# Moving the query projections of an attention stage ahead, and its output transfers to GpSimd's DMA queue

## The chip, the cores and the metric

The kernel runs on one core of a Trainium2 chip. Its engines are TensorE (PE; its weight loads are shown apart as PEld), VectorE (DVE), ScalarE (ACT), GpSimd (POOL) and SyncE (SP), which here only issues DMAs. Each engine executes its own instructions in order and waits at semaphores for the others. The metric is the time of one execution on the device in microseconds, as a median of several runs.

## The reference

Two stages follow one another. The first is attention without a softmax: queries and keys are sketched into 64 features, which are products of two projections to 8 each. The second is a mixture of eight experts whose routing weights come from eight Sinkhorn iterations.

```python
# q, k, v: (4 batches, 4 heads, 1088, 32); S1, S2: (8, 32)
def phi(x):
    a = np.einsum('rd,bhsd->bhsr', S1, x)
    b = np.einsum('rd,bhsd->bhsr', S2, x)
    return np.einsum('bhsi,bhsj->bhsij', a, b).reshape(*x.shape[:-1], 64)
q_p, k_p = phi(q), phi(k)
kv = np.einsum('bhsf,bhsd->bhfd', k_p, v)
z = np.sum(k_p, axis=2)
num = np.einsum('bhsf,bhfd->bhsd', q_p, kv)
den = np.einsum('bhsf,bhf->bhs', q_p, z)[..., None] + 1e-06
x = (num / den)               # -> (4352, 128): one row for each batch and position

logits = x @ w_gate           # (4352, 8)
P = np.exp(logits - logits.max())
for _ in range(8):            # rows, then columns
    P /= P.sum(1, keepdims=True) + 1e-09
    P /= P.sum(0, keepdims=True) + 1e-09
    P *= N / E
for e in range(8):            # w1[e]: 128 x 1024, w2[e]: 1024 x 128
    out += P[:, e:e + 1] * (np.maximum(x @ w1[e], 0.0) @ w2[e])
```

All is in float32.

## The kernel before

The experts' matrix products make up most of the work, and they are cut into small steps. A generator `steps()` puts out one step at a time, and `fill(n)` takes steps from it until about n units of work are out; a step on 480 columns counts as one unit, one on 256 columns as 0.53. The attention is put out piece by piece with calls of `fill` between the pieces, so that TensorE has expert work while the attention waits for VectorE, ScalarE or a DMA. The order on TensorE and VectorE is the order of these calls. Experts 0 and 1 are applied without routing weights to some of the rows at first (their results are weighted later); these steps need only x.

Step by step, the order from the start is as follows (cut to what matters):

```python
with tc.manual_schedule(engines={engines.DVE, engines.PE, engines.Activation}):
    ...
    transpose_k(0)
    keys_ab(0)                    # projects the keys
    ...
    keys_sums(0)
    multiply(0)
    transpose_q(0, chunks[0][1])
    keys_kept(0)
    query_products(1)
    fractions(0)
    multiply(1)
    divide(0)                     # writes x of batch 0, columns 0 to 384
    fractions(1)
    query_products(2)
    divide(1)
with tc.manual_schedule(engines={engines.DVE, engines.PE}):
    fill(1)
    multiply(2)
    fractions(2)
    fill(1)
    transpose_q(1)
    queries_ab(1)
    repeat_a(1)
    repeat_b(1)
    fill(1)
    divide(2)
    fill(1)
    transpose_k(1)
    load_k(2)
    load_q(2)
    load_v(2)
    fill(1)
    keys_ab(1)
    fill(1.5)
    keys_products(1, 0)
    fill(1.5)
    keys_products(1, 1)
    fill(1.5)
    keys_products(1, 2)
    fill(1.5)
    for b in range(1, B):
        for n, _ in zip((1.4,) * (9 if b + 1 < B else 5), attention(b), strict=True):
            fill(n)
    for n in routing():           # begins with fill(5), then the logits of all batches
        fill(n)
```

Batches 1 to 3 take their queries a longer way. They are transposed (VectorE), projected (TensorE, 12 matmuls; line 418), copied from PSUM (ScalarE; line 421), written to DRAM repeated (tiles qa and qb, two and four DMAs; lines 425 and 429), and read back into ph (four DMAs; line 434) and rb (one DMA; line 437), so that one elementwise product of ph and rb makes the 64 features:

```python
def transpose_q(b, lo=0, hi=S):
    nc.vector.transpose(out=qT[:, lo:hi], in_=loaded["q", b]...[:, lo:hi])      # L288

def queries_ab(b):
    ...
    x = qT.rearrange("p (h q c t s) -> p h c t q s", h=2, q=2, c=3, t=3)
    for cs in ((0, 1), (2,)):
        ...
        nc.tensor.matmul(...)                                                   # L418
        nc.scalar.copy(ab[:, cs[0]:cs[-1] + 1], pq)                             # L421
    ...
    nc.sync.dma_start(out=qa[:, :, s], in_=x)                                   # L425, two of them
    ...
    nc.sync.dma_start(out=qb[h, :, :, s]..., in_=x)                             # L429, four

def repeat_a(b):
    for j in range(4):
        nc.sync.dma_start(out=phs[b % 2][j::4], in_=queries[b][0]...)           # L434

def repeat_b(b):
    nc.sync.dma_start(out=rb, in_=queries.pop(b)[1]...)                         # L437

def times(b, c):
    ph = third(phs[b % 2], c)
    nc.vector.tensor_tensor(ph, ph, third(rb, c), op=Alu.mult)                  # L444
```

The attention of one batch from 1 on, with the output's way: `tops` multiplies features and key sums (L453), `over` divides and transposes (L466 to L472), and `take_over` turns the result into the layout of x through DRAM:

```python
def take_over(b, lo, hi):
    xd = dram.tile([P, H, hi - lo], F32, name=f"xd{b}{lo}")
    nc.sync.dma_start(out=xd, in_=turned[b][:, :, lo:hi])                       # L477
    for h in range(H):
        nc.sync.dma_start(out=xT[32 * h:32 * (h + 1), ...], in_=xd...[h])       # L479

def attention(b):
    follows = b + 1 < B
    keys_sums(b)
    times(b, 0)
    if follows:
        transpose_q(b + 1)
    yield
    keys_kept(b)
    if follows:
        queries_ab(b + 1)
        repeat_a(b + 1)
    times(b, 1)
    tops(b, 0)
    yield
    times(b, 2)
    if follows:
        repeat_b(b + 1)
    over(b, 0)
    tops(b, 1)
    yield
    over(b, 1)
    if b + 1 == B:
        take_over(b, 0, 192)
    yield
    tops(b, 2)
    if follows:
        transpose_k(b + 1)
    ...                           # loads of batch b + 2
    yield
    over(b, 2)
    ...                           # take_over of the rest, then the keys of batch b + 1
```

The keys are transposed into kT (L292, L294) and projected from there (L303, L307). The expert work's first layer is L889, its second L1062; L906 and L951 are VectorE's sums between the two. The logits' matmuls are L487. PSUM tiles named "a" rotate through four banks.

Of the kernel before, what the change touches and what calls it, by code (L numbers as in the profile page):

```python
# [10 lines left out]
F32 = mybir.dt.float32  # L11
# [39 lines left out]
def kernel(  # L51
# [12 lines left out]
    nc = tc.nc  # L64
    P = nc.NUM_PARTITIONS
    B, H, S, D = q.shape
# [58 lines left out]
    xT = big.tile([P, N + 2 * 32], F32, name="xT")  # L125

    W9 = 9 * 32
    qT = wk.tile([P, 4 * W9], F32, name="qT", bufs=1)
    nc.gpsimd.memset(qT[:, S:], 0.0)
    kT = wk.tile([P, S], F32, name="kT", bufs=1)  # L130

    phs = [wk.tile([P, 2, 4 * W9], F32, name=f"ph{i}", bufs=1) for i in range(2)]
    rb = wk.tile([P, 2, 4 * W9], F32, name="rb", bufs=1)

    lgT = qT[:, 0:S].rearrange("p (a s) -> p a s", s=32)
    lgp = kT.rearrange("p (a e) -> p a e", e=32)
    pT = dram.tile([E, N], F32, name="pT")


# [24 lines left out]
    def load_q(b):  # L164
        qx = ld.tile([P, SA, D], F32, tag="q", name="qx")
        nc.sync.dma_start(out=qx, in_=q[b].rearrange("h (s a) d -> (h s) a d", a=SA))
        loaded["q", b] = qx

    def load_v(b):
        vx, o = v_slots[b % 2], v[b].offset  # L170
        for c in range(4):
            nc.sync.dma_start(
                out=vx[32 * c:32 * (c + 1), 0:H, 0:NT, :].rearrange("p h t d -> p h (t d)"),
                in_=AP(tensor=v.tensor, offset=o + NT * D * c, ap=[[SA * D, 32], [S * D, H], [1, NT * D]]))
        for c in range(2):
            nc.sync.dma_start(
                out=vx[32 * c:32 * (c + 1), 0:H, NT, :],
                in_=AP(tensor=v.tensor, offset=o + (4 * NT + c) * D, ap=[[SA * D, 32], [S * D, H], [1, D]]))

    load_k(0)  # L180
    load_q(0)
    load_v(0)

    def load_w(e, sums=True, again=False):
        w1 = wpool.tile([P, F], F32, tag="w1", name="w1")
# [92 lines left out]
    nc.gpsimd.memset(wg, 0.0)  # L278
    nc.sync.dma_start(out=wg[:, 0:E], in_=moe_w_gate)
    first_w = load_w(0)  # L280
    load_q(1)
    load_v(1)


    keys, queries = {}, {}

    def transpose_q(b, lo=0, hi=S):
        nc.vector.transpose(out=qT[:, lo:hi], in_=loaded["q", b].rearrange("p a d -> p (a d)")[:, lo:hi])  # L288

    def transpose_k(b):  # L290
        kx = loaded["k", b]
# [79 lines left out]
    def multiply(c):  # L371
        lo, hi = chunks[c]
        for i, pb in enumerate(queries[0, c]):
            nc.vector.tensor_tensor(phs[0][:, i, lo:hi], phs[0][:, i, lo:hi], pb, op=Alu.mult)
# [34 lines left out]
    def queries_ab(b):  # L409
        qa = dram.tile([H * R, 2, 2, 2 * W9], F32, name=f"qa{b}")  # L410
        qb = dram.tile([2, R, 2 * R, 2, 2 * W9], F32, name=f"qb{b}")
        ab = wk.tile([P, 3, 192], F32, tag="qab", name="qab", bufs=1)
        x = qT.rearrange("p (h q c t s) -> p h c t q s", h=2, q=2, c=3, t=3)
        for cs in ((0, 1), (2,)):
            pq = bank()[:, 0:192 * len(cs)].rearrange("p (c n) -> p c n", n=192)
            for i, c in enumerate(cs):
                for s in range(2):
                    nc.tensor.matmul(pq[64 * s:64 * (s + 1), i].rearrange("p (t q s) -> p t q s", t=3, q=2),  # L418
                                     wdq.rearrange("p n f -> p (n f)"), x[:, s, c], start=True, stop=True,
                                     tile_position=(0, 64 * s))  # L420
            nc.scalar.copy(ab[:, cs[0]:cs[-1] + 1], pq)  # L421
        abf = ab.rearrange("p c n -> p (c n)")
        for s in range(2):
            x = abf[64 * s:64 * s + 32].unsqueeze(1).to_broadcast([32, 2, 2 * W9])
            nc.sync.dma_start(out=qa[:, :, s], in_=x)  # L425
        for s in range(2):
            for h in range(2):
                x = abf[64 * s + 32 + h:64 * (s + 1):2].unsqueeze(1).to_broadcast([2 * R, R, 2 * W9])
                nc.sync.dma_start(out=qb[h, :, :, s].rearrange("i f n -> f i n"), in_=x)  # L429
        queries[b] = qa, qb  # L430

    def repeat_a(b):
        for j in range(4):
            nc.sync.dma_start(out=phs[b % 2][j::4], in_=queries[b][0].rearrange("(x r) j s n -> (r j) x (s n)", x=2))  # L434

    def repeat_b(b):
        nc.sync.dma_start(out=rb, in_=queries.pop(b)[1].rearrange("h i (j x) s n -> (h i j) x (s n)", x=2))  # L437
# [4 lines left out]
# [4 lines that stand above are left out]
    def tops(b, c):  # L446

        pn = bank()[:, 0:3 * H * (D + 1)].rearrange("p (t h d) -> p t h d", t=3, h=H)
        ph = third(phs[b % 2], c)
        for t in range(3):  # L450
            for i in range(2):
                for s in range(2):
                    nc.tensor.matmul(pn[64 * s:64 * (s + 1), t, 2 * i:2 * i + 2].rearrange("p h d -> p (h d)"),  # L453
                                     ph[:, i, s, 64 * t:64 * (t + 1)], kvs[b % 2][:, i].rearrange("p h d -> p (h d)"),
                                     start=(t == 0 and i == 0), stop=False, tile_position=(0, 64 * s))
        for s in range(2):
            nc.tensor.matmul(pn[64 * s:64 * (s + 1), :, :, D], ones[:, 0:64], eps, start=False, stop=True,
                             tile_position=(0, 64 * s))
        queries[b, c] = pn
# [14 lines left out]
    def take_over(b, lo, hi):  # L474

        xd = dram.tile([P, H, hi - lo], F32, name=f"xd{b}{lo}")
        nc.sync.dma_start(out=xd, in_=turned[b][:, :, lo:hi])  # L477
        for h in range(H):
            nc.sync.dma_start(  # L479
                out=xT[32 * h:32 * (h + 1), b * S:b * S + 4 * W9].rearrange("d (f n) -> d f n", f=4)[:, :, lo:hi],  # L480
                in_=xd.rearrange("(f d) h n -> h d f n", f=4)[h])

# [15 lines left out]
    def attention(b):  # L498


        follows = b + 1 < B
        keys_sums(b)
        times(b, 0)
        if follows:
            transpose_q(b + 1)
        yield
        keys_kept(b)
        if follows:
            queries_ab(b + 1)
            repeat_a(b + 1)  # L510
        times(b, 1)
        tops(b, 0)
        yield
        times(b, 2)
        if follows:
            repeat_b(b + 1)
        over(b, 0)
# [8 lines that stand above are left out]
            transpose_k(b + 1)  # L526
        if b + 2 < B:
            load_k(b + 2)
            load_q(b + 2)
            load_v(b + 2)  # L530
        yield
        over(b, 2)
        if b + 1 < B:
            take_over(b, 0, W9)
        else:
            take_over(b, 192, W9)
        if follows:
            keys_ab(b + 1)
            yield
            keys_products(b + 1, 0)  # L540
            yield
            keys_products(b + 1, 1)
            yield
            keys_products(b + 1, 2)
            yield
# [589 lines left out]
    with tc.manual_schedule(engines={engines.DVE, engines.PE, engines.Activation}):  # L1135
        st = projections()
        transpose_k(0)
        keys_ab(0)
        repeated(st)
        load_k(1)  # L1140
        transpose_q(0, 0, chunks[0][1])
        query_products(0)
        for part_ in range(3):
            keys_products(0, part_)
        keys_sums(0)
        multiply(0)
        transpose_q(0, chunks[0][1])
        keys_kept(0)
        query_products(1)
        fractions(0)  # L1150
        multiply(1)
        divide(0)
        fractions(1)
        query_products(2)
# [3 lines that stand above are left out]
        multiply(2)  # L1158
        fractions(2)
        fill(1)  # L1160
        transpose_q(1)
        queries_ab(1)
        repeat_a(1)
        repeat_b(1)
        fill(1)
        divide(2)
        fill(1)
        transpose_k(1)
        load_k(2)
        load_q(2)  # L1170
        load_v(2)
        fill(1)
        keys_ab(1)
        fill(1.5)
        keys_products(1, 0)
        fill(1.5)
        keys_products(1, 1)
        fill(1.5)
        keys_products(1, 2)
        fill(1.5)  # L1180
        for b in range(1, B):
            for n, _ in zip((1.4,) * (9 if b + 1 < B else 5), attention(b), strict=True):
                fill(n)
        for n in routing():
            fill(n)
        early.close()
        pools.append(ctx.enter_context(tc.tile_pool(name="late", bufs=2)))
        prepare_x(PLAIN)
        fill(8)
# [32 lines left out]
```

## Time and profile before

| | us |
|---|---|
| time, median of 3 runs | 940.04 |
| lowest and highest | 938.84, 941.04 |
| span of the profiled execution | 935.3 |
| TensorE busy | 914.8 |
| VectorE busy | 696.3 |
| ScalarE busy | 416.6 |
| GpSimd busy | 195.9 |

In the profile, a line of a timeline gives the start and the length in microseconds, the engine, the line of the kernel, the operation, the tiles written and read, and how many instructions were merged into it; in square brackets stands the idle time ahead of it and what ended that. SPq stands for SyncE's queue of DMA issues. In a list of waits, the numbers are the total, the count and the longest. The row of slices cuts the span into 40 equal parts and gives the busy share of each in tenths. The mean granted clock of TensorE is 0.998. The attention occupies the first 122 us, the routing the time to about 185 us, and from there the weighted expert work runs to the end.

### The profile page before, as it was taken

How to read it: one execution, taken by the hardware profiler on the slowest of the kernel's cores; microseconds unless marked ns; L12 is line 12 of the kernel's file. 1: busy time of each engine (PE TensorE's matmuls, PEld its weight loads, DVE VectorE, ACT ScalarE, POOL GpSimd, SP SyncE). 2: the span in 40 equal slices, each digit the busy share in tenths (PEclk: the TensorE clock that was granted, in tenths of full speed). 3: DMA queues.
4: the chain of work that ended last, by engine and by line, in shares of the span. 5: the costliest groups of instructions: out<-in, count | busy, mean ns of one | idle time of the engine just before them, and what ended most of it. 6: DMA issues, size and time to landing. Idle time of an engine off the chain costs nothing.

```text
span 935.3 us, 18858 instructions
## 1 busy us (share of the span) xinstructions
PE 914.8 (98%) x7434; PEld 556.6 (60%) x7434; DVE 696.3 (74%) x1200; ACT 416.6 (45%) x901; POOL 195.9 (21%) x182
## 2 busy tenths in 40 slices
PE   8888999999999999999999999999999999999997
PEld 6676634666666666665555555555555555556864
DVE  7687769978788788586876656965757977768655
ACT  2544345564444454434544444544445444445443
POOL 2010000073665501130020101201110343321210
PEclk9999999999999999999999999999999999999999
DMA  7896300123335545354354534364434446442640
GB/s 216 226 290 166 113 21 1 26 105 108 107 109 170 172 148 151 121 174 142 117 154 121 179 107 148 111 182 131 140 115 152 151 150 204 160 167 92 183 140 12
DMA packets 93208, 128.14 MB, mean 137 GB/s; under 512 B 25376, under 2 KB 71456, under 8 KB 88384
## 3 DMA queue, kind: packets, MB, share of 16 engines
q1 hardware_dynamic: 91888, 126.78, 43.8%
q8 instruction: 58, 0.95, 0.4%
q10 hardware_dynamic: 1232, 0.16, 0.1%
q14 instruction: 30, 0.25, 0.1%
HBM read 107.88 MB, written 19.05 MB: 136 GB/s over the span
## 4 chain that ended last, share of the span: by engine, by line
PE 90%; DVE 8%; issue 1%; ACT 1%; POOL 0%; DVEq 0%; ACTq 0%; POOLq 0%
PE a L889 47%; PE s L1062 40%; DVE hb L906 2%; PE a L335 1%; PE a L114 1%; PE a L303 0%; PE a L453 0%; DVE rs L582 0%; DVE ph L444 0%; DVE p L585 0%; DVE cs L588 0%; DVE kp L319 0%; DVE kept L715 0%; DVE w L718 0%; DVE kT L292 0%
## 5 line engine op out<-in xcount | busy, mean ns | idle before, releaser
L889 PE MATMUL a<-xe,w 128*64 128x256 f32 (+1 forms) x2560 | 517.5, 470 | 0.0
L893 ACT ACTIVATE hb<-a 128x256 f32<-128x256 f32 (+5 forms) x408 | 194.9, 479 | 253.5 <-PE a L889 225.0
L893 ACT ACTIVATE hx<-a 128x256 f32<-128x256 f32 (+1 forms) x360 | 167.1, 464 | 213.9 <-PE a L889 194.1
L889 PEld LDWEIGHTS a<-xe,w 128*64 128x64 f32 x2560 | 206.8, 137 | 79.8
L1062 PE MATMUL s<-hb,ws 128*64 128x256 f32 (+4 forms) x1344 | 237.8, 395 | 2.4 <-DVE hb L906 1.6
L1062 PE MATMUL s<-hx,ws 128*64 128x256 f32 x1280 | 204.8, 379 | 0.6 <-DVE kept L718 0.6
L951 DVE TENSOR_TENSOR hb<-hb 128x512 f32<-128x512 f32 (+1 forms) x204 | 133.4, 665 | 93.9 <-ACT hb L893 89.8
L951 DVE TENSOR_TENSOR hx<-hx 128x512 f32<-128x512 f32 (+1 forms) x204 | 153.3, 761 | 66.3 <-ACT hx L893 61.1
L658 POOL TENSOR_TENSOR xe<-xT,xe 128x768 f32<-128x768 f32 (+2 forms) x41 | 85.1, 2076 | 554.5 <-DMA xe<-pT 401.6
L1062 PEld LDWEIGHTS s<-hb,ws 128*64 128x64 f32 x1344 | 113.8, 137 | 110.6 <-issue 80.0
L1062 PEld LDWEIGHTS s<-hx,ws 128*64 128x64 f32 x1280 | 105.9, 137 | 99.7 <-issue 74.4
L889 PE MATMUL a<-xT,w 128*64 128x480 f32 (+4 forms) x512 | 119.4, 463 | 3.7 <-DVE hb L906 2.5
L1062 PE MATMUL s<-hb,w 128*64 128x256 f32 (+4 forms) x496 | 101.9, 410 | 0.0
L906 DVE TENSOR_TENSOR hb<-hb 128x480 f32<-128x480 f32 (+8 forms) x96 | 64.2, 670 | 21.1 <-ACT hb L893 13.6
L1062 PE MATMUL s<-hx,w 128*64 128x256 f32 x384 | 68.3, 379 | 0.0
L889 PEld LDWEIGHTS a<-xT,w 128*64 128x64 f32 x512 | 50.5, 137 | 26.6 <-issue 14.2
L238 POOL TENSOR_TENSOR ws<-w 128x256 f32<-128x256 f32 (+1 forms) x70 | 60.1, 892 | 13.6 <-PE a L889 8.7
L1062 PEld LDWEIGHTS s<-hb,w 128*64 128x64 f32 x496 | 45.8, 137 | 22.8 <-issue 8.1
L906 DVE TENSOR_TENSOR hx<-hx 128x256 f32<-128x256 f32 (+1 forms) x65 | 39.1, 607 | 24.5 <-ACT hx L893 23.4
L951 DVE TENSOR_TENSOR pqg<-hb 128x512 f32<-128x512 f32 x68 | 48.8, 759 | 0.0
L1062 PEld LDWEIGHTS s<-hx,w 128*64 128x64 f32 x384 | 34.0, 137 | 10.9 <-DVE hx L906 0.3
L951 DVE TENSOR_TENSOR pqg<-hx 128x512 f32<-128x512 f32 x68 | 35.8, 566 | 0.0
(164 smaller groups left out, 468.8 us busy)
## 6 DMA issues: line engine op xcount, KB each, us to landing
w<-in_moe_w_dram SPq DMA_DIRECT2D x82, 512.0 KB, 5.0
ws<-ws SPq DMA_DIRECT2D x34, 1024.0 KB, 4.9
xe<-pT SPq DMA_DIRECT2D x34, 384.0 KB, 4.0
ws<-ws SPq DMA_DIRECT2D x12, 512.0 KB, 4.9
qb<-qab SPq DMA_DIRECT2D x12, 288.0 KB, 4.2
ph<-qa SPq DMA_DIRECT2D x12, 288.0 KB, 4.4
rb<-qb SPq DMA_DIRECT2D x3, 1152.0 KB, 8.0
pb<-pT SPq DMA_DIRECT2D x6, 384.0 KB, 6.7
```

The source lines that it names most:

```text
L114: nc.tensor.matmul(warm[:, 0:P], ones, ones, start=True, stop=True)
L238: tc.keep_in_program_order(nc.gpsimd.tensor_tensor(ws[:, c:c + len(ns)], blocks(x), blocks(y), op=Alu.subtract if off else Alu.add))
L335: nc.tensor.matmul(pv[64 * s:64 * (s + 1), i], kp[0:n, H * t + h].rearrange("p i j -> p (i j)"), vx[0:n, slots[h], t, :], start=(t == 0 an ...
L658: tc.keep_in_program_order(nc.gpsimd.tensor_tensor(out, x, pb, op=Alu.mult))
L889: nc.tensor.matmul(ph[sl], loaded_w[j][0][:, P * f + H2 * s:P * f + H2 * (s + 1)], sources[j][:, lo:hi], start=True, stop=True, tile_posit ...
L893: nc.scalar.activation(out=out, in_=ph, func=Act.Relu)
L906: nc.vector.tensor_tensor(out, a, b, op=Alu.subtract)
L951: nc.vector.tensor_tensor(out if not isinstance(out, tuple) else places(*out), places(*a), places(*b) if isinstance(b, tuple) else b, op=A ...
L1062: nc.tensor.matmul(sums[g][i][H2 * s:H2 * (s + 1), n * place:n * (place + 1)], w, x, start=c == 1, stop=c == per, tile_position=(0, H2 * s))
```

## The change

Every batch's queries are projected earlier, and the output of the attention is moved by another queue.

- Batch 1's queries are loaded ahead of the first expert weights, transposed during batch 0 and put into kT, the keys' buffer, which is free at that time. They are projected, and their repeated copies sent on their way, between batch 0's second multiplication and its first division.
- Batch 2's queries are transposed after batch 1's first `tops` and projected after its third `times`, instead of at the start of that attention. Batch 3's follow later in batch 1's attention, between the products of batch 2's keys, instead of in batch 2's.
- x is carried by DMAs that GpSimd issues, not SyncE.
- The calls of `fill` before the attention of batch 1 come to 7.5 units instead of 11, and the keys of batch 1 are transposed ahead of the last division of batch 0.

The aim is to have the repeated queries in place when they are wanted, and to keep x's transfers from standing in SyncE's queue behind DMAs that wait.

```diff
-    qT = wk.tile([P, 4 * W9], F32, name="qT", bufs=1)
-    nc.gpsimd.memset(qT[:, S:], 0.0)
-    kT = wk.tile([P, S], F32, name="kT", bufs=1)
+    qT, kT = (wk.tile([P, 4 * W9], F32, name=n, bufs=1) for n in ("qT", "kT"))
+    for t in (qT, kT):
+        nc.gpsimd.memset(t[:, S:], 0.0)
 ...
     load_v(0)
+    load_q(1)
 ...
     first_w = load_w(0)
-    load_q(1)
     load_v(1)
 ...
     def transpose_q(b, lo=0, hi=S):
-        nc.vector.transpose(out=qT[:, lo:hi], in_=...)
+        to = kT if b == 1 else qT
+        nc.vector.transpose(out=to[:, lo:hi], in_=...)
 ...
-        x = qT.rearrange("p (h q c t s) -> p h c t q s", h=2, q=2, c=3, t=3)
+        x = (kT if b == 1 else qT).rearrange("p (h q c t s) -> p h c t q s", h=2, q=2, c=3, t=3)
 ...
-        nc.sync.dma_start(out=xd, in_=turned[b][:, :, lo:hi])
+        nc.gpsimd.dma_start(out=xd, in_=turned[b][:, :, lo:hi])
         for h in range(H):
-            nc.sync.dma_start(
+            nc.gpsimd.dma_start(
 ...                                    # attention(b)
         times(b, 0)
-        if follows:
-            transpose_q(b + 1)
         yield
         keys_kept(b)
-        if follows:
-            queries_ab(b + 1)
-            repeat_a(b + 1)
         times(b, 1)
         tops(b, 0)
+        if b == 1:
+            transpose_q(2)
         yield
         times(b, 2)
+        if b == 1:
+            queries_ab(2)
+            repeat_a(2)
         if follows:
             repeat_b(b + 1)
 ...
             load_k(b + 2)
-            load_q(b + 2)
             load_v(b + 2)
 ...
             keys_products(b + 1, 0)
+            if b == 1:
+                transpose_q(3)
             yield
             keys_products(b + 1, 1)
+            if b == 1:
+                queries_ab(3)
+                repeat_a(3)
 ...                                    # the order from the start
         keys_kept(0)
+        transpose_q(1)
         query_products(1)
         fractions(0)
         multiply(1)
+        queries_ab(1)
+        load_q(2)
+        repeat_a(1)
+        repeat_b(1)
         divide(0)
 ...
         fractions(2)
         fill(1)
-        transpose_q(1)
-        queries_ab(1)
-        repeat_a(1)
-        repeat_b(1)
-        fill(1)
-        divide(2)
-        fill(1)
         transpose_k(1)
         load_k(2)
-        load_q(2)
         load_v(2)
+        load_q(3)
+        divide(2)
+        fill(1.5)
+        keys_ab(1)
         fill(1)
-        keys_ab(1)
-        fill(1.5)
         keys_products(1, 0)
-        fill(1.5)
+        fill(1)
         keys_products(1, 1)
-        fill(1.5)
+        fill(1)
         keys_products(1, 2)
-        fill(1.5)
+        fill(1)
```

More of the change, by code (lines that the diff above doesn't have):

```diff
@@ L135 @@
     lgT = qT[:, 0:S].rearrange("p (a s) -> p a s", s=32)
-    lgp = kT.rearrange("p (a e) -> p a e", e=32)
+    lgp = kT[:, 0:S].rearrange("p (a e) -> p a e", e=32)
     pT = dram.tile([E, N], F32, name="pT")
@@ L287, in transpose_q @@
     def transpose_q(b, lo=0, hi=S):
-        nc.vector.transpose(out=qT[:, lo:hi], in_=loaded["q", b].rearrange("p a d -> p (a d)")[:, lo:hi])
+        to = kT if b == 1 else qT
+        nc.vector.transpose(out=to[:, lo:hi], in_=loaded["q", b].rearrange("p a d -> p (a d)")[:, lo:hi])
     def transpose_k(b):
```

## The prediction

> **What bounds the kernel now.** I read the page's busy times first, then its row of slices, then TensorE's waits by stretch, and only then the timelines of the stretches in which TensorE stood still.
>
> ```profile
> PE 914.8 (98%) x7434; PEld 556.6 (60%) x7434; DVE 696.3 (74%) x1200; ACT 416.6 (45%) x901; POOL 195.9 (21%) x182
> PE   8888999999999999999999999999999999999997
> DMA  7896300123335545354354534364434446442640
> ```
>
> TensorE is idle for 935.3 - 914.8 = 20.5 us in all. The chain that ended last runs through TensorE for 90% of the span. Asked in stretches, TensorE has no idle time from 230 to 900 us and loses 7.6 us of 36 in the tail; neither is touched. Everything that the change moves lies before 130 us, where the slices (23.4 us each) show 8s. The number of matmuls stays the same, so the change can only give back idle time. The list of waits from 40 to 125 us holds all of it there:
>
> ```profile
> PE a L889 <- DVE hb L906: 2.5, 1, 2.5
> PE a L303 <- DVE kT L294: 1.4, 1, 1.4
> PE a L453 <- ACT qab L421: 1.3, 1, 1.3
> PE a L418 <- ACT f L736: 1.2, 1, 1.2
> ```
>
> That is 6.4 us; from 20 to 40 us there are 0.86 (for the second piece of x of batch 0), 0.2 and 0.89 us (for the keys' transpose) more. So about 8 us, 0.9% of 940, is the ceiling. The releasers named are the last by time, not always the cause. Three timelines show the causes (VectorE, then SyncE's queue; columns are start, length, what):
>
> ```profile
> 43.84 0.96 DVE L444 TENSOR_TENSOR ph<-ph,rb 128x768 f32<-128x768 f32 x1 [5.28 <-DMA rb<-qb]
> 44.72 1.30 DVE L288 STREAM_TRANSPOSE qT<-qx 128x1088 f32<-128x1088 f32 x1
> ```
> ```profile
> 67.72 0.34 SPq L477 DMA_DIRECT2D xd<-xt  x1
> 77.52 0.60 SPq L425 DMA_DIRECT2D qa<-qab  x1
> 78.23 2.41 SPq L479 DMA_DIRECT2D xT<-xd  x4
> ...
> 116.05 0.55 SPq L477 DMA_DIRECT2D xd<-xt  x1
> 118.57 1.74 SPq L479 DMA_DIRECT2D xT<-xd  x4
> ```
> ```profile
> 83.73 1.03 PE L889 MATMUL a<-xT,w 128*64 128x480 f32 x4 [2.55 <-DVE hb L906]
> ...
> 122.02 2.24 PE L487 MATMUL a<-xT,wg 128*32 128x384 f32 x24
> ```
>
> VectorE sits 5.28 us for the repeated queries of batch 1 (rb) to land. Then the transpose for batch 2's queries stands ahead of everything else, ends at 46.02, and the projection (L418) starts at 46.17: its 1.25 us is this transpose's, not ScalarE's. The products after it (L453, at 48.67) wait for the copy of the key sums, which VectorE ends at 48.57. On SyncE's queue, x of batch 1 leaves for DRAM at 67.72, and the four DMAs that bring it back go out only at 78.23: ahead of them stands an issue that waits 9.5 us for qab. They land 3.2 us after the last one, issued at 80.2, which is 83.5, and the first matmul on batch 1's x starts at 83.73. So this wait of 2.55 us is x's, though the view names hb.
>
> **What the skill says.** "Perfetto Trace Analysis", section Optimization Strategy, says to look for gaps on the contended engine and follow each to the semaphore behind it; this trace agrees in so far as all the gaps above lead to VectorE's order or to SyncE's. "DMA: Bandwidth & Descriptors", section Issuing engines are not separate DMA queues, says that another issuing engine gets no bandwidth of its own, only saves issue time. In the trace the 9.5 us is lost in the order of issue while the DMA engines carry next to nothing (share 0.13 from 70 to 80 us), so the move can help. The same page, section Latency and other measured facts, gives about 1 us to the first byte from GpSimd's queue against 0.6 us from SyncE's. The kernel before issues nothing on GpSimd's queue, so no run here shows it. It is the one new cost.
>
> **The change part by part.**
>
> First, batch 1's queries. The transpose (1.30 us, L288) goes behind the copy of batch 0's key sums, which ends at 13.92 on VectorE, where VectorE waits 1.35 us until 15.27: it fits. It needs batch 1's queries by then; they are now the fourth load instead of one behind the weights, some 2.2 MB in, 11 us at the 201 GB/s of the first 10 us. The projection (1.20 us on TensorE) goes in front of the second fraction, about 16.5 to 17.7; the second fraction's last bank is then free only when batch 0's first division ends, at 18.46. The third query products follow from 19.2 to 20.6, so the expert work starts at 20.6 instead of 19.14. But the 0.86 us wait for x's second piece at 20.65 is gone, and so are the later projection and the wait of 0.89 us, because the keys' transpose now precedes the last division. I put the end of batch 1's key projection at 26.5 us, against 30.4 now with 1.5 units more of fill done (three steps, about 2.2 us): a gain of 1.6 us. Against it, VectorE now has from 21.8 us on the transpose (1.4), the division (2.2), the key products (2.85) and three blocks of sums (4.8): 11.3 us, to 33.1, while TensorE would want the products at 32.5. I charge 0.6 us.
>
> Second, rb of batch 1. The chain from the first issue (25.49) to its landing (43.84) is 18.35 us, mostly transfers. Begun at 18.2, it lands at 36.5. But the fill before attention of batch 1 falls from 11 to 7.5 units, so that attention starts near 32.5 instead of 39.2, and the two move almost together. The products L453 came 4.83 us behind rb; without the transpose 3.5, so 40.0; TensorE arrives at about 38.1. The gap of 1.25 + 1.30 becomes 1.9 or so, and with the contention of batch 2's load 2.2. Gain 0.3 us.
>
> Third, batch 2's transpose and projection go behind those products. The wait of 1.39 us before L303 at 61 has a VectorE that is nearly always busy from 43.8 to 61; its work is the same, but TensorE now has 1.2 us more to do in the same stretch. Gain 0.6 us, the least certain of these.
>
> Fourth, x on GpSimd's queue. GpSimd does nothing between 55.4 and 193.7 us, so x of batch 1 is not held up: out at some 57, back by 66, with the first use near 80. Gain 2.5 us, the whole wait. For batch 3 it is the reverse. Its second part goes out at 116.05, comes back with issues from 118.57, and its last DMA, issued at 119.9, lands 2.1 us later at 122.0; the logits start at 122.02. That has no slack, and TensorE executes in order. Two stages in a row at 0.4 us later first byte are 0.8 us (estimate from the skill's two figures), and five issues that take perhaps 0.3 us more each than SyncE's 0.43 add 1.2 (a guess). I charge 2.0 us.
>
> Sum: -1.6 + 0.6 - 0.3 - 0.6 - 2.5 + 2.0 = -2.4 us, so 940.0 - 2.4 = 937.6. Attention's earlier start makes routing earlier as well, but the work without routing weights is a fixed amount, so this only gives slack before the weighted part.
>
> **The rivals.**
>
> *All gaps close, x on GpSimd costs nothing.* Then 8 us go, less the 0.6: 932 or so. For it speaks that GpSimd's queue is empty and that its transfers are small (576 KB, 384 KB and 192 KB). Against it that rb and attention move together.
>
> *GpSimd issues slowly.* Had each of the four returning DMAs 1.2 us of issue instead of 0.43 and the first part stood in the queue ahead of the second, the logits would wait 5 to 7 us: 941 to 943. Nothing in the profile speaks against it, since no DMA there starts from GpSimd.
>
> *Batch 2's repeated queries become the new wait.* Their projection comes later in attention of batch 1 (about 44.7 by my clock) while attention of batch 2 comes some 6.5 us earlier, near 64.5. With the 18 us of the chain, rb lands at 63 and is wanted at about 66. If the loads of batch 3 and the next weights push it back (the DMA share is 0.96 to 1.00 from 30 to 70 us), VectorE waits again: up to 3 us, 940.
>
> **Range and chances.** The gains together lie between 2 and 8 us, the costs between 0 and 7. Taking them as independent gives about 932 to 943 for 8 in 10. Faster by 2% would be 18.8 us, more than twice the idle time in reach; slower by 2% would need a wait of about 19 us on a chain that now takes some 6, or a cost of GpSimd's queue elsewhere that nothing here shows. So 0.01, 0.97 and 0.02.
>
> **What would show it.** In the changed profile: the 2.55 us before the first 480-column matmul gone, with x of batch 1 issued back within about 4 us of leaving; a wait of 1 to 4 us before L487's counterpart, released by a DMA of xT; VectorE's wait for rb 3 to 4 us instead of 5.28; still some 2 us before L453's counterpart. I am wrong if TensorE's idle time before 130 us is under 6 us (the first rival) or if the logits wait over 5 us (the second), or if time is lost after 230 us.

## The result, and the profile after

The changed kernel takes 935.27 us (median of four executions, 934.94 to 936.09) against 939.44 us for the kernel before beside it: a ratio of 0.9956, with a 95% interval from 0.9938 to 0.9975. Run once more later, with 22 executions against 35 of the kernel before, it came to 0.9969 (0.9960 to 0.9979). So it is faster by 0.2 to 0.6%, some 2 to 6 us; the second measurement, the tighter one, puts it near 2.9 us. Part of that goes with the granted clock (the last section). The profiled executions differ by 2.3 us (spans 935.3 and 933.0), at the same mean clock of 0.998.

From the page of the changed kernel, the busy times, TensorE's row of slices, and the queue that GpSimd's DMAs now use:

```profile
PE 914.5 (98%) x7434; PEld 588.2 (63%) x7434; DVE 693.6 (74%) x1200; ACT 416.9 (45%) x901; POOL 206.2 (22%) x203
PE   8999899999999999999999999999999999999997
q0 software_dynamic: 1168, 3.54, 1.3%
```

TensorE's busy time and its 7434 matmuls are as before; its idle time went from 20.5 to 18.5 us. Of the four slices that were 8 the first still is, the other three have become 9, and the fifth, from 93 us, has become 8. TensorE's list of waits from 40 to 125 us, which had four lines, has these five as its largest:

```profile
PE a L488 <- issue: 2.5, 1, 2.5
PE a L894 <- DVE rd L469: 0.9, 1, 0.9
PE a L454 <- DVE rd L469: 0.8, 1, 0.8
PE a L304 <- DVE kT L295: 0.7, 1, 0.7
PE a L454 <- ACT m L735: 0.6, 1, 0.6
```

The line numbers have moved: L894 was L889, L454 was L453, L488 was L487, L304 was L303. No wait has kept its old size. The waits of at least 0.2 us, added up by stretch from the timelines of both kernels:

| stretch, us | waits before, us | waits after, us |
|---|---|---|
| 20 to 40 | 0.86 + 0.24 + 0.89 = 1.99 | 0.25 |
| 40 to 80 | 1.25 + 1.30 + 1.39 = 3.94 | 0.80 + 0.24 + 0.86 + 0.56 + 0.26 = 2.72 |
| 80 to 100 | 2.55 | 0.71 |
| 100 to 130 | 0 | 2.50 + 1.59 = 4.09 |
| 130 to 230 | 0.87 + 0.72 + 0.77 + 0.61 = 2.97 | 0.75 + 0.22 = 0.97 |
| sum | 11.45 | 8.74 |

The sum falls by 2.7 us; the span falls by 2.3. Added up by stretch, 6.8 us went and 4.1 us came. The largest new one lies inside the logits' matmuls. Its timeline (TensorE), and GpSimd's queue and VectorE ahead of it:

```profile
112.07 0.85 PE L488 MATMUL a<-xT,wg 128*32 128x384 f32 x6
115.42 1.99 PE L488 MATMUL a<-xT,wg 128*32 128x384 f32 x18 [2.50 <-issue]
```
```profile
54.52 0.73 POOL L478 DMA_DIRECT2D xd<-xt  x1 [6.45 <-DVE kept L720]
63.95 2.20 POOL L480 DMA_DIRECT2D xT<-xd  x4 [8.70 <-DMA xd<-xt]
...
106.14 2.20 POOL L480 DMA_DIRECT2D xT<-xd  x4 [3.31 <-DMA xd<-xt]
108.33 0.76 POOL L478 DMA_DIRECT2D xd<-xt  x1
111.25 2.20 POOL L480 DMA_DIRECT2D xT<-xd  x4 [2.16 <-DMA xd<-xt]
```
```profile
104.23 0.58 DVE L473 STREAM_TRANSPOSE xt<-rd 128x384 f32<-128x384 f32 x1
```

Six of the 24 logits instructions run, those on x of batches 0 to 2; then TensorE stands until the last part of batch 3's x has landed. That part is ready at 104.81, when the transpose ends, but GpSimd issues it only at 108.33: its queue is in order, and ahead of it stand the first part's four returning DMAs, which wait for that part's own way through DRAM until 106.14. The four for the second part go out from 111.25 to 113.45 and land 2.1 us after their issue in the median. Batch 1's x, on the other hand, leaves at 54.52, is sent back from 63.95, and is used first at 79.01: the 2.55 us are gone.

VectorE still waits for batch 1's repeated queries, though less:

```profile
35.23 0.96 DVE L445 TENSOR_TENSOR ph<-ph,rb 128x768 f32<-128x768 f32 x1 [2.49 <-DMA rb<-qb]
```

### The profile page after: what moved, and what is told of

Same layout as the page of the kernel before. It is cut to its first block, busy times and chain, and to the rows that moved or that the text cites. A ratio compares the mean times of both kernels' runs of the same rounds, so it can differ in the third digit from the quotient of the medians.

```text
span 933.0 us, 18870 instructions
## 1 busy us (share of the span) xinstructions
PE 914.5 (98%) x7434; PEld 588.2 (63%) x7434; DVE 693.6 (74%) x1200; ACT 416.9 (45%) x901; POOL 206.2 (22%) x203
## 4 chain that ended last, share of the span: by engine, by line
PE 88%; DVE 6%; DMA 2%; issue 2%; ACT 1%; POOL 1%; SPq 0%; DVEq 0%; ACTq 0%; POOLq 0%
PE a L894 46%; PE s L1067 39%; DVE hb L911 1%; DMA xd<-xt 1%; POOL xT L480 1%; PE a L336 1%; DMA kx<-in_k_dram 0%; PE a L384 0%; DVE kT L293 0%; DMA ph<-qa 0%; DVE cs L593 0%; PE a L454 0%; PE s L366 0%; DVE kp L320 0%; DVE rs L587 0%
## 5 line engine op out<-in xcount | busy, mean ns | idle before, releaser
L894 PE MATMUL a<-xe,w 128*64 128x256 f32 (+1 forms) x2560 | 525.8, 470 | 0.0
L894 PEld LDWEIGHTS a<-xe,w 128*64 128x64 f32 x2560 | 220.4, 137 | 65.2 <-issue 1.3
L1067 PE MATMUL s<-hb,ws 128*64 128x256 f32 (+4 forms) x1344 | 241.1, 395 | 1.0 <-DVE hb L911 1.0
L1067 PE MATMUL s<-hx,ws 128*64 128x256 f32 x1280 | 208.7, 379 | 0.2 <-DVE kept L723 0.2
L956 DVE TENSOR_TENSOR hx<-hx 128x512 f32<-128x512 f32 (+1 forms) x204 | 150.1, 745 | 71.2 <-ACT hx L898 66.1
L956 DVE TENSOR_TENSOR hb<-hb 128x512 f32<-128x512 f32 (+1 forms) x204 | 131.0, 653 | 93.4 <-ACT hb L898 89.5
L1067 PEld LDWEIGHTS s<-hb,ws 128*64 128x64 f32 x1344 | 119.6, 137 | 101.9 <-issue 73.7
L1067 PEld LDWEIGHTS s<-hx,ws 128*64 128x64 f32 x1280 | 112.7, 137 | 91.1 <-issue 70.5
L894 PE MATMUL a<-xT,w 128*64 128x480 f32 (+4 forms) x512 | 122.5, 464 | 1.1 <-DVE rd L469 0.9
L894 PEld LDWEIGHTS a<-xT,w 128*64 128x64 f32 x512 | 52.0, 137 | 25.3 <-issue 10.9
L1067 PEld LDWEIGHTS s<-hb,w 128*64 128x64 f32 x496 | 47.8, 137 | 24.2 <-issue 6.5
```

What stands on the lines that cost most here:

```text
L894: nc.tensor.matmul(ph[sl], loaded_w[j][0][:, P * f + H2 * s:P * f + H2 * (s + 1)], sources[j][:, lo:hi], start=True, stop=True, tile_posit ...
L956: nc.vector.tensor_tensor(out if not isinstance(out, tuple) else places(*out), places(*a), places(*b) if isinstance(b, tuple) else b, op=A ...
L1067: nc.tensor.matmul(sums[g][i][H2 * s:H2 * (s + 1), n * place:n * (place + 1)], w, x, start=c == 1, stop=c == per, tile_position=(0, H2 * s))
```

## The experiments

Every ratio is against executions of the kernel before on the same chip. Executions of one and the same kernel spread by up to 7 us (the kernel before: 934.96 to 942.50 in 46), so the medians of different sets are not compared with one another directly, only the ratios, and what single waits are worth is read from the profiles. The runs lie on three chips: e1, e2, e3 and e5 on the first; e0_again, e4_second_sync, e8 and b2 on the second; e4_again, e6, b3 and b4 on the third. Only the second set has the changed kernel itself beside its variants.

The theory at the start was this: TensorE's work is fixed, the time is that work and its waits; the new order of the queries is what helps; x on GpSimd's queue removes one wait and brings another, by the order of that queue. The rivals: GpSimd's queue is the main gain; or its DMAs are slow in themselves; or a wait before the logits is made up for later.

**All of x on SyncE's queue in the new order (e1_x_sync).**

```diff
-        nc.gpsimd.dma_start(out=xd, in_=turned[b][:, :, lo:hi])
+        nc.sync.dma_start(out=xd, in_=turned[b][:, :, lo:hi])
 ...
-            nc.gpsimd.dma_start(
+            nc.sync.dma_start(
```

> The changed kernel with x's DMAs back on SyncE's queue, all else as changed. Theory: once the queries are projected earlier, SyncE's queue holds nothing that keeps x from where it is wanted; batch 1's x comes back by about 75 us against a first use near 78, and batch 3's two parts no longer stand one behind the other on GpSimd, so the wait of 2.5 us before the logits goes: about 2.5 us under the changed kernel (0.993 of the kernel before). Rival: the move to GpSimd's queue is what brought the gain, as it took away the wait of 2.55 us for batch 1's x; then this run is about 2.5 us slower than the changed kernel (0.998).

Measured: 934.54 us, ratio 0.9961 (0.9948 to 0.9973). The rival falls: no wait for batch 1's x has come back, so in the new order that transfer doesn't need GpSimd. But the 2.5 us of the theory aren't there either; the ratio overlaps with the changed kernel's. The logits wait 0.84 us in place of 2.50, and the profiled execution had lost time elsewhere, in a part that the edit doesn't touch: 2.11 us before the first products, after which the granted clock fell to 0.83 from 40 to 50 us (1.00 there in the changed kernel). VectorE's and TensorE's timelines of that run:

```profile
38.23 0.96 DVE L445 TENSOR_TENSOR ph<-ph,rb 128x768 f32<-128x768 f32 x1 [4.90 <-DMA v<-in_v_dram]
```
```profile
40.15 1.16 PE L454 MATMUL a<-kvs,ph 128*64 128x66 f32 x24 [2.11 <-issue]
```

The same read of rb, issued at 27.54 as in the changed kernel (27.56), lets VectorE go on at 38.23 and not at 35.23, with the same program up to there. (The view names the load of v; the read of rb itself landed 10.7 us after its issue, which is 38.2.) So the landing of rb varies by 3 us between executions, and TensorE's wait behind it by nearly 2.

**Only x moved to GpSimd's queue, in the kernel before (e2_x_gp_only).** The edit is the reverse of the one above, made in the kernel before.

> The kernel before with only x's DMAs moved to GpSimd's queue. Theory: the wait of 2.55 us for batch 1's x goes and one of about 2.5 us before the logits comes, so 0.999 to 1.001 of the kernel before. Rival: the queue is the main gain of the change, then about 0.996. In the profile: no idle time before the first 480-column matmul, 2 to 3 us in the middle of the logits' matmuls.

Measured: 936.64 us, ratio 0.9977 (0.9966 to 0.9987), a gain between the theory's and the rival's. In the profile the 2.55 us are gone and the logits wait 1.52 us, less than the 2.5 expected: its second part stood in GpSimd's queue for 1.3 us (ready at 113.55, issued at 114.86), not for 3.5. The three waits that hang on VectorE's order are all still there (1.48, 1.30 and 1.38 us). So each part alone is worth 0.2 to 0.4% by these ratios, and the two don't add up: both remove the 2.55 us. In e2's profile the waits from 20 to 230 us fall by only 0.8 us, less than the 2.1 us of its ratio.

**Both parts of batch 3 on SyncE's queue (e3_last_sync), and batch 3 as one part on GpSimd's (e5_one_part).**

```diff
+        queue = nc.sync if b == B - 1 else nc.gpsimd       # e3
-        nc.gpsimd.dma_start(out=xd, ...)
+        queue.dma_start(out=xd, ...)                       # and the four others
```
```diff
-        if b + 1 == B:                                     # e5
-            take_over(b, 0, 192)
 ...
-        if b + 1 < B:
-            take_over(b, 0, W9)
-        else:
-            take_over(b, 192, W9)
+        take_over(b, 0, W9)
```

> The changed kernel, x of batches 1 and 2 on GpSimd's queue, both parts of batch 3 on SyncE's. Theory: the wait of 2.5 us before the logits goes and nothing else changes: 2.5 us under the changed kernel, 0.993 of the kernel before. Rival: the logits' wait is made up for by a wait that comes later anyway (VectorE's order in the routing), then within 0.7 us of the changed kernel.

> The changed kernel, batch 3's x on GpSimd's queue as one part instead of two. Theory: what costs is the order of the queue (the second part is ready at 104.8 us but is issued at 108.3, behind the first part's wait for its own way through DRAM); as one part it leaves at 104.8, comes back with issues from about 108.3 and lands at about 113, so the logits wait 0.5 us or less: 2 us under the changed kernel. Rival: GpSimd's issues are slow in themselves (0.55 us each against 0.43), so that joining the parts saves nothing or costs: within 0.5 us of the changed kernel or slower.

Measured: 934.10 us, 0.9954 (0.9935 to 0.9974), and 934.39 us, 0.9955 (0.9942 to 0.9968). The logits wait 0.55 and 0.41 us. That one part on GpSimd's queue lands in time speaks against slow DMAs as the main cost and for the order of the queue. By their profiles both gain 2 us in this stretch and keep it: the first store of results goes out at 354.77 and 354.75 us, against 356.82 in the changed kernel. Their ratios, though, lie only 0.15% under the second, tighter one of the changed kernel, and the intervals overlap.

**The changed kernel again (e0_again), and only the second part of batch 3 on SyncE's queue (e4_second_sync, e4_again).**

```diff
+        queue = nc.sync if lo else nc.gpsimd
-        nc.gpsimd.dma_start(out=xd, ...)
+        queue.dma_start(out=xd, ...)                       # and the four others
```

> The changed kernel once more, unaltered, as a yardstick beside the other runs on the same chip. Its first measurement was 0.9956 of the kernel before from four executions. Expected 0.995 to 0.997. If the wait of 2.5 us before the logits counts in full, the runs without it (0.9954, 0.9955) should stand 0.2% under this one, so this one should come at 0.9975 or so; if it doesn't count, at 0.9955.

> The changed kernel, only the second part of batch 3's x on SyncE's queue, the first part on GpSimd's. Theory: the cost of GpSimd's queue was that the second part stood behind the first's wait; with two queues it goes out at about 105 us, lands at about 111.5, and the logits wait 0.5 us or less: 2 us under the changed kernel of this call. Rival: GpSimd's slower issues; then the first part alone, which lands at about 110.5, changes nothing and the saving is under 1 us, with a wait of 1.5 us left.

> The changed kernel with only the second part of batch 3's x on SyncE's queue, once more, to narrow its 0.9936 (0.9916 to 0.9957). Expected 0.993 to 0.995, under the changed kernel's 0.9969 (0.9960 to 0.9979); if the logits' wait of 2.4 us counts, by 0.25%.

Measured: the changed kernel 936.36 us, 0.9969 (0.9960 to 0.9979); with the second part on SyncE's queue 933.43 us, 0.9936 (0.9916 to 0.9957), and again, on the third chip, 932.92 us, 0.9920 (0.9902 to 0.9937). The intervals don't overlap: the wait counts. SyncE's queue, the returned second part and the logits in the second of these runs (timelines of two engines):

```profile
105.25 0.57 SPq L479 DMA_DIRECT2D xd<-xt  x1
108.94 1.75 SPq L481 DMA_DIRECT2D xT<-xd  x4
```
```profile
112.50 2.04 PE L489 MATMUL a<-xT,wg 128*32 128x384 f32 x24
```

VectorE's transpose ends at 105.22 and the part leaves at 105.25, with nothing before it in its queue; the logits' 24 instructions follow each other without a gap. Two in-order queues do what one couldn't.

In the second profile of the changed kernel the wait before the logits cost more than its length. The 18 logits matmuls after it took 3.25 us instead of 1.99. Its line, then the windows of 110 to 120 us of this profile and of the first one (busy time of PE, PEld, DVE, ACT and POOL in us, then clock, DMA share and GB/s):

```profile
115.83 3.25 PE L488 MATMUL a<-xT,wg 128*32 128x384 f32 x18 [2.45 <-DMA xT<-xd]
```
```profile
110.00:120.00 10.00, 7.55 (x40) 2.34 (x38) 3.94 (x7) 1.14 (x2) 2.20 (x4) 0.83 0.15 41
```
```profile
110.00:120.00 10.00, 7.50 (x48) 2.51 (x46) 3.63 (x7) 1.48 (x3) 2.20 (x4) 1.00 0.12 29
```

The wait of 1.59 us near 129 us is not bound to the logits' wait. Both runs of e4 lack the latter and have the former, as have e3 and e5 (TensorE's timeline of e4_again):

```profile
126.20 0.62 PE L1068 MATMUL s<-hb,w 128*64 128x480 f32 x1 [1.58 <-DVE kept L724]
```

**Batch 3's queries projected in batch 2's attention (e8_q3_later).** The conditions `if b == 1` for batch 2 become `if follows`, and the lines for batch 3 go.

```diff
-        if b == 1:
-            transpose_q(2)
+        if follows:
+            transpose_q(b + 1)
 ...
-        if b == 1:
-            queries_ab(2)
-            repeat_a(2)
         if follows:
+            queries_ab(b + 1)
+            repeat_a(b + 1)
             repeat_b(b + 1)
 ...
-            if b == 1:
-                transpose_q(3)
 ...
-            if b == 1:
-                queries_ab(3)
-                repeat_a(3)
```

> The changed kernel with batch 3's queries transposed and projected in batch 2's attention (after the first products and after the third multiplication) and not already in batch 1's. Theory: VectorE is the bound from 36 to 62 us and the transpose of 1.3 us and the projection there bring the waits of 0.86 and 0.24 us before 62; they shrink by about 0.9 us, but rb of batch 3 lands later, near 91 us instead of 85, and VectorE waits some 2 us for it, of which TensorE sees up to 1: within 1 us of the changed kernel. Rival: the early projection of batch 3 is a real part of the gain, then 2 to 4 us slower.

Measured: 935.59 us, 0.9962 (0.9948 to 0.9977), not to be told from the changed kernel. VectorE waits 1.65 us for rb of batch 3 and TensorE loses nothing by it, but the waits of 0.86 and 0.24 us that were to shrink are unchanged; those of 0.26 and 0.71 near 76 and 82 us went instead. The expected sum was right and its account wrong: the early projection of batch 3 is not what makes the waits before 62 us, and it is no measurable part of the gain. Its profile, too, has a clock of 0.83 from 110 to 120 us, after a wait of 2.34 us, and the 18 logits matmuls take 3.66 us.

**Batch 2's keys and values loaded later (b2_late_kv).** With batch 3's x as one part, the two loads move from before `divide(2)` to just before the loop over the batches.

> The changed kernel with batch 3's x as one part, and with batch 2's keys and values loaded just before batch 1's attention and so behind the queries of batch 3 on SyncE's queue, which wait there until rb of batch 1 has landed. Theory: rb (1.15 MB) lands 7.7 us after its issue because these loads share the 16 DMA engines with it (share 1.0, 400 GB/s from 30 to 35 us); without them it lands at about 32.5 and VectorE's wait of 2.5 us goes, TensorE's 0.25 us too: 0.3 to 1 us under the run with one part, and less spread between executions. Rival: rb's time is its own chain of issues, so nothing moves; or the loads now fall on batch 2's chain and its rb comes after 62 us, then 1 to 3 us slower.

Measured: 933.47 us, 0.9941 (0.9922 to 0.9960), its interval overlapping with e5's. The experiment didn't do what it was for: the load of batch 3's queries, which was to hold the queue until rb had landed, went out at once (28.41), and the moved loads behind it from 28.88 to 35.90, while rb was still under way. VectorE waited 1.85 us for rb. Whether those transfers delay rb stays open; the DMA share is about 1 from 30 to 40 us in both profiles, and the run never took the loads away from there.

**The fill as before (e6_fills_old).**

```diff
-        fill(1.5)
+        fill(3)
         keys_ab(1)
-        fill(1)
+        fill(1.5)                      # and the three after each of the key products
```

> The changed kernel with 11 units of fill before batch 1's attention, as in the kernel before, instead of 7.5. Theory: the fill is the same work in another place; attention starts some 5 us later, so VectorE does not wait for rb of batch 1 any more (0 instead of 2.2 to 4.9 us) and the wait of TensorE that hangs on it (0.25 us in most executions, 2.1 in one) goes; everything after is shifted but equal: within 1 us of the changed kernel, rather faster. Rival: the earlier attention is part of the gain, since it gives batch 1's x time before its first use; then a wait returns before the first 480-column matmul and the time is 1 to 3 us longer.

Measured: 932.94 us, 0.9916 (0.9896 to 0.9937), clear of the changed kernel's interval (0.9960 to 0.9979), though that was measured on another chip; e4_again, beside it, has 0.9920. Its executions had a higher clock (0.999) than those of the kernel before beside them (0.995 on average), so less than the whole 0.5% is the fill's. The waits settle the sign: from 20 to 230 us they come to 5.45 us, against 8.74 in the changed kernel, and the first store of results goes out at 353.94 us, not at 356.82. This part of the change costs, some 3 us. TensorE's waits from 20 to 125 us in this run, all of them:

```profile
PE a L488 <- DMA xT<-xd: 1.5, 1, 1.5
PE a L454 <- ACT hb L898: 0.5, 1, 0.5
PE a L304 <- DVE kT L295: 0.3, 1, 0.3
PE a L894 <- DVE xT L403: 0.2, 1, 0.2
```

The five waits between 40 and 80 us, 2.72 us in the changed kernel, are down to 0.47 + 0.30, the 0.71 at 82 is gone, and VectorE no longer waits for a DMA anywhere from 30 to 130 us. The rows of 40 to 60 us from the windows of the kernel before, the changed kernel, and this run (columns as before):

```profile
40.00:60.00 20.00, 17.24 (x251) 13.18 (x245) 14.45 (x27) 8.26 (x22) 3.93 (x4) 1.00 0.99 282
```
```profile
40.00:60.00 20.00, 18.10 (x225) 12.82 (x223) 17.91 (x32) 9.57 (x26) 3.96 (x5) 1.00 0.91 264
```
```profile
40.00:60.00 20.00, 19.23 (x256) 15.34 (x252) 16.79 (x32) 10.00 (x27) 4.70 (x5) 1.00 0.68 186
```

In the changed kernel VectorE is 90% busy here, and TensorE waits for it again and again. With the fill as before, VectorE has less to do in the stretch (16.79 us for 17.91) and TensorE does 1.1 us more work. It isn't the time that VectorE lost to rb just before: that is 1.85 us in b2, 2.49 in the changed kernel and 3.42 in e4_second_sync, and TensorE's waits between 40 and 80 us add up to 2.36, 2.72 and 2.73 us. What of the moved fill relieves VectorE was not taken apart further.

The fill also sets the waits after attention. The logits wait 1.53 us, a microsecond less, as the second part of x stands only 1.7 us in GpSimd's queue (ready at 109.19, issued at 110.86). And from 124 to 230 us the waits follow the fill in every run. With 7.5 units there is one of 1.58 to 1.60 us between 124 and 132 us, then one of some 0.7 and one of 0.2 to 0.35. With 11 units (the kernel before, e2 and e6) the first is 0.86 or 0.87 us, and three of 0.6 to 0.8 follow. The first of e6:

```profile
130.68 0.62 PE L1067 MATMUL s<-hb,ws 128*64 128x480 f32 x1 [0.86 <-DVE hb L911]
```

**A version faster than both (b3_over_first, b4_over_late).** Both build on e4. In b3 the first division of each attention goes ahead of the third multiplication on VectorE; b4 also has the later loads of b2.

```diff
         yield
+        over(b, 0)
         times(b, 2)
 ...
             repeat_b(b + 1)
-        over(b, 0)
         tops(b, 1)
```

> As e4, and in each attention the first division (over) goes ahead of the third multiplication on VectorE. Theory: the wait of 0.8 us before the second products at 43 us is for the PSUM bank of the first ones, which VectorE frees only after that multiplication (0.96 us); it goes, while the multiplication is wanted later: 0.5 to 1 us under e4. Rival: the multiplication now frees rb 1.4 us later, batch 2's repeated queries come later by as much and VectorE waits for them: no gain.

> As b3_over_first, and batch 2's keys and values loaded behind batch 1's rb. Theory: both savings add up, 1 to 1.5 us under e4 (0.992 of the kernel before). Rival: the loads delay batch 2's chain and cost what they save.

Measured: 932.55 us, 0.9912 (0.9893 to 0.9930), and 931.50 us, 0.9902 (0.9885 to 0.9919). The wait of 0.8 us at 43 us is gone in both profiles, as it should be if it was for the bank that this division frees. Against e4_again beside them (0.9920) the intervals overlap; b4 has the lowest ratio of all, not to be told from b3's or e6's, and clearly under the changed kernel's, though measured on another chip. Its gain over b3 can't be put to the later loads: VectorE waited 2.83 us for rb in it. The fill as before together with e4's two queues and this order wasn't tried.

## Why the prediction was right, and where it wasn't

It said 937.6 us, from 940.0, with 932 to 943 as its range, and "same" at 0.97. The measured change, -4.2 us at first and 0.31% or -2.9 us with more executions, compares with its -2.4. By its terms (waits read from the profiles):

**What bounds the kernel.** Right in the main: the gain and the loss lie in TensorE's waits, and nothing was lost from 230 to 900 us. But they don't all lie before 130 us, as it said: those from 130 to 230 fell by 2.0 us. The tail's 7.6 us of 36 were counted past the span's end; up to 935.3 us it is 6.9.

**Batch 1's queries early.** Right in kind and near in size. The transpose fits where it was put (13.75 to 15.06), the expert work starts at 19.90 (20.6 was said), the key projection starts at 25.25 and is done near 26.4 (26.5). The charge of 0.6 us for a VectorE that would be late with the key products was not needed: the key sums start at 31.85 without a wait. The 2.0 us of waits in this stretch are gone, where the term left a net gain of 1.0.

**rb of batch 1.** Mechanism right, size off. "Begun at 18.2, it lands at 36.5" came to a start at 17.85 and a landing at 35.2, and the products came 2.5 us after that, not 3.5. VectorE's wait, for which 3 to 4 us were said, was 2.49. The gap that should have been 2.2 us was 0.25 in the profiles of the changed kernel, 0.6 in e4's and 2.11 in e1's. So this term was worth 2.3 us rather than 0.3, and it varies between executions.

**Batch 2's transpose and projection.** This step failed: "Gain 0.6 us, the least certain of these". From 40 to 62 us 1.90 us of waits stand where it left 0.8, and from 62 to 82 there are 1.53 us more that the kernel before didn't have: a loss of 2.0 us (1.90 + 1.53 - 1.39). The prediction had VectorE's work unchanged and left it there. What it took for neutral, the 3.5 units less of fill, is the cause, as e6 shows: with it put back, 0.77 us are left from 40 to 82 us of the 3.43. Which part of the fill's place matters to VectorE stays open. This more than cancels the error in the term before.

**x on GpSimd's queue.** Batch 1's wait went as said, 2.55 us. One sign failed: x was to be issued back within about 4 us of leaving and took 9.4 (54.52 to 63.95), with the DMA engines at a share of 0.89 to 1.07 from 54 to 64 us. It cost nothing, as the first use came at 79.01. The loss for batch 3 was put at 2.0 and measured 2.50 (2.45 in the second profile, 2.34 in e8). The reason given was only part of it (and five issues at 0.3 us more would be 1.5 us, not 1.2). GpSimd's four issues take 2.20 us against 1.74 from SyncE, and from the second part's issue to the first return it takes 2.92 us against 2.52: 0.9 us. The larger part is what stood under the rivals, "the first part stood in the queue ahead of the second", 3.5 us from ready to issued, as e4 and e5 show. That the wait is smaller than the two together is because x of batch 3 is now ready 7.3 us before the logits (104.81 and 112.07), where it was 6.2 before (115.79 and 122.02).

The Trainium skill says in "DMA: Bandwidth & Descriptors", section Issuing engines are not separate DMA queues, that another issuing engine only saves the time of issuing. The measurement differs here. What the move changed is which waits stand ahead in an in-order queue: 2.55 us less on TensorE for batch 1's x, and 3.5 us of standing for the second part of batch 3's.

**Routing.** Waits from 130 to 230 us fell from 2.97 to 0.97 us, but one of 1.59 came just before 130, together 0.4 us less. The prediction saw only slack here. Both go with the fill, as said under e6.

So the sum was right partly by luck, as errors of opposite sign met: 3.0 us too little gain for batch 1's queries and rb (1.0 and 2.0), 2.6 us too much for the step after them.

## What to carry to other kernels

Where an engine is saturated, a change of order is worth what it takes from that engine's waits; list them by stretch before and after, for the gain often comes back as other waits. Moving DMAs off a crowded in-order queue helps as far as nothing ahead of them in the new queue waits; a transfer in two legs blocks its own successor, and two queues, or one part instead of two, cured that here. And work that fills in for a wait isn't neutral in its place: taking 3.5 units of it from in front of the attention cost here some 3 us by the waits, more than the 2.3 us that the earlier rb had won.

## What the runs showed of the hardware

GpSimd's DMA issues took 0.55 us each for the four that return x, against 0.43 us on SyncE's queue, and 0.56 to 0.76 us for those that send it; 21 more entries of GpSimd (182 to 203) raised its busy time by 10.3 us. A read of 1.15 MB from DRAM, issued at the same moment in the same program (27.56 and 27.54 us), let VectorE go on after 7.7 us in one execution and after 10.7 in another.

The time goes with the granted clock. Of the 46 executions of the kernel before on the first chip, the five at 0.993 have a median of 941.5 us and the seven at 0.998 one of 936.8, so 0.001 is 0.9 us, as much as most of these waits. The kernels that are faster here also had the higher clocks: on the second chip 0.9963 on average for the kernel before, 0.9972 for the changed one. A straight line fitted to all these executions of the three chips, with one constant for each chip and for each kernel, puts the changed kernel 2.2 us under the kernel before at equal clock, e2 1.0 us and e6 4.8 us, with some 0.5, 0.5 and 1.1 us of uncertainty (an estimate). For e2 and e6 that is nearer to what their waits lost (0.8 and 6.0 us) than the ratios are (2.1 and 7.9 us).

The clock may itself follow from the waits. In the 14 profiles it falls below 1.00 between 0 and 920 us in three only (e0_again, e1 and e8), each time right after TensorE has waited 2.1 to 2.5 us. The kernel before and the changed kernel's first profile have waits of 2.5 us without it, and the nine profiles whose waits from 20 to 230 us are all under 1.7 us don't have it. That the waits cause it is not shown.
